# VectorE's and ScalarE's work in attention tied to program order, with three steps moved

## The chip, the cores and the metric

The kernel runs on one core of one Trainium2 chip. The metric is the device time of one execution in microseconds. The kernel before takes 2076.37 us (median of three runs, 2076.05 to 2076.4). The engines are named as in the profile: PE is TensorE (matrix products), DVE is VectorE, ACT is ScalarE, POOL is GpSimd, SP is the queue that starts DMA transfers. PSUM is the memory that TensorE writes its products to; it is divided into banks of 128 x 512 f32.

## The reference

The input x has 2048 rows of 640 numbers. Two kinds of layer alternate, each twice, each added to what went into it:

```
x = x + A(layernorm(x));  x = x + B(layernorm(x))
x = x + A(layernorm(x));  x = x + B(layernorm(x))

A(x):  a = x @ hid_re.T;  b = x @ hid_im.T           # Fourier transform over the columns
       y = seq_re @ a - seq_im @ b                   # and over the rows, real part
B(x):  q, k, v = x @ wqkv                            # 32 heads of 20
       s = q @ k.T * 20 ** -0.5
       s = where(0 <= row - col < 256, s, -1e9)      # each row sees itself and the 255 rows before it
       o = softmax(s) @ v;  return o @ wo
```

The Fourier matrices are inputs; A is computed as plain matrix products.

## The kernel before, in words

Large products are made of f16 parts: each operand is split into a high and a low f16 half, and three products of halves are added in PSUM. The program runs four stages, one after the other: spectral 0, attention 0 (555.8 to about 1073 us of the profiled span), spectral 1, attention 1 (from 1580.2 us to the end).

**Attention's loop.** It turns over pairs of heads and row tiles (`for G in range(NS // 2 + 1)`); one turn is called a visit here. There are 128 visits with scores, and a short tail. In a visit TensorE makes, in this order:

- the far scores of four heads of a 128-row tile (the key tile that lies two tiles back; 4 products into `sk`), which are needed for their maxima only;
- the transposed scores (`by_key`, key rows on the partitions) of the pair that was scored 8 visits ago, 12 products into the rest of `sk`; the exponential reads these, and by now they contain the negated row maximum as two more rows of the product;
- the near scores (8 products into `sq`);
- in even visits the two transposes of `back`, which turn a finished block of outputs (12 visits after its scores), and in odd visits one transpose of `hand_on` (the maxima of two visits as rows, 3 visits later) and the 32 products with v (`values`, 11 visits later);
- one unit of other work of 15 products: a projection of q, k or v, or a tile of the output product with wo. Units are 256 or 320 columns wide. A planner with due times chooses which.

VectorE's part is `largest(G, pi)` for pi 0 and 1, a copy and a reduce each: the copy (L1155) writes the far scores over those near ones that the mask takes out, so that one reduce (L1157) finds the maximum over all 256 columns. `back` adds a reciprocal (L1258, of the sums) and a multiply (L1259, into `o`) in even visits. ScalarE's part is `probabilities`, two exponentials (L1210, first pi = 1, then pi = 0), and copies out of PSUM: `ht` (L1175, the turned maxima, then sent to memory and back into the rows of q), `pvs` (L1242, the products with v), `qf` (L365) and `v` (L881, projections). GpSimd masks the exponentials and splits into halves.

In the background there are slow steps, one in an even visit and two in an odd one: the norm of rows for a later block (`norm_steps`: statistics L139 and L142, a square root by small operations on 128 x 1 numbers L148 to L152, the norm `lny` L166), ScalarE's f16 copy of it (L177, `rx`), and, in attention 0, the split of wo. The out tile adds into x by VectorE (L935).

**Where it lies in PSUM.** `sq` is one bank for each pi, `sk` two banks for each pi. The far scores are the first 256 columns of `sk`, the transposed scores the other 768, so that far scores and a part of the exponential's input share a bank. A ring of two banks (`pf`) serves everything else: back, hand_on, values and the units. Each waits until the reader of the bank two turns earlier is through.

**What sets the order.** TensorE's instructions and SP's transfers follow the order in which the program writes them (`tensor` and `load` chain them with `tc.issue_after` while `in_turn[0]` holds, that is in attention). GpSimd's are put in order by the scheduler. So are VectorE's and ScalarE's, but for a few ties: `in_line("dve")` ties each copy and each reduce, and the first operation of `back`, behind the last of VectorE's marked instructions, `in_line("act")` does the same for the exponentials, and a slow step comes behind the visit's last reduce (`topped`).

Of the kernel before, what the change touches and what calls it, by code (L numbers as in the profile page):

```python
# [72 lines left out]
def body(ctx: ExitStack, tc: tile.TileContext, x_in, cmat, whid, wqkv, wo, out):  # L73
# [55 lines left out]

    matmul, transpose = partial(tensor, "matmul"), partial(tensor, "transpose")  # L130

    def norm_steps(xs, ys, act=False):
# [3 lines left out]
        for k, x in enumerate(xs):  # L136
            st = keep.tile([P, 2, 6], F32, tag="lnst", name="lnst", bufs=2)
            for h in range(2):
                nc.vector.bn_stats(st[:, h], x[:, h * 320:(h + 1) * 320])  # L139
                if h == 0:  # L140
                    yield
            nc.vector.bn_aggr(mv[:, k], st.rearrange("p a b -> p (a b)"))  # L142
            yield
        t = keep.tile([P, 3, n], F32, tag=f"lnt{n}", name="lnt", bufs=2)
        ts = nc.vector.tensor_scalar
# [14 lines left out]
        for k, x in enumerate(xs):  # L160
            g, u = t[:, 1, k:k + 1], t[:, 2, k:k + 1]
            y = keep.tile([P, D], F32, tag="lny", name="lny", bufs=2)
            if act:
                nc.scalar.activation(y, x, AF.Identity, bias=u, scale=g)
# [11 lines left out]
    def split(hi, lo, y, eng):  # L176
        nc.scalar.activation(hi, y, AF.Copy)  # L177
        eng.tensor_tensor(lo, y, hi, op=OP.subtract)
# [45 lines left out]
    class Hidden:  # L224
# [29 lines left out]
        def stage(self, s, pool, new=new_f):  # L254
# [23 lines left out]
            def parts(m, f):  # L278
                nc.scalar.activation(zc[:, m, 0], f, AF.Copy)
                nc.gpsimd.tensor_tensor(zc[:, m, 1], f, zc[:, m, 0], op=OP.subtract)  # L280

            def scaled(o):
                nc.scalar.activation(o, z, AF.Copy, scale=Z_DOWN)

            def minus(o, f):
                nc.vector.scalar_tensor_tensor(o, z, Z_DOWN, f, op0=OP.mult, op1=OP.subtract)
# [42 lines left out]
    class Projections:  # L329
# [19 lines left out]
        def qk(self, b, w, ct):  # L349
# [15 lines left out]
            nc.scalar.activation(f, pf[:, :QB], AF.Copy, scale=down)  # L365
# [13 lines left out]
    def spectral(layer, res_src, hidden, first):  # L379
        with ExitStack() as st:  # L380
# [40 lines left out]
            def split_w(n, f):  # L421
                c, dt = divmod(n, ND)
                up = -C_UP if c else C_UP
                marks["act"] = nc.scalar.activation(w[:, 0, c, dt], f, AF.Copy, scale=up).ins
                marks["dve"] = nc.vector.scalar_tensor_tensor(w[:, 1, c, dt], f, up, w[:, 0, c, dt],
                                                              op0=OP.mult, op1=OP.subtract).ins

            def transposed(xs, k, xt):
# [3 lines left out]
                if k:  # L432
                    nc.vector.tensor_copy(xt[:, k], pt)
                else:
                    nc.scalar.activation(xt[:, k], pt, AF.Copy)
# [81 lines left out]
            def take_c(n):  # L517
# [13 lines left out]
                def high(m, f):  # L531
                    cc[m] = sb.tile([P, 2, RS * P], F16, tag="cc", name="cc", bufs=14)
                    nc.scalar.activation(cc[m][:, 0], f, AF.Copy, scale=C_UP)  # L533

                def low(m, f):
                    nc.vector.scalar_tensor_tensor(cc[m][:, 1], f, C_UP, cc[m][:, 0], op0=OP.mult, op1=OP.subtract)  # L536
# [21 lines left out]
            def add(o, z, f):  # L558
                marks["dve"] = nc.vector.scalar_tensor_tensor(o, z, Y_DOWN, f, op0=OP.mult, op1=OP.add).ins  # L559
# [12 lines left out]
            def main_a(r, j):  # L572
# [5 lines left out]
                marks["act"] = nc.scalar.activation(f[:, 0], z, AF.Copy, scale=Y_DOWN).ins  # L578
# [87 lines left out]
            def b_max():  # L666
# [3 lines left out]
                for n in range(20):  # L670
                    nc.vector.tensor_reduce(wmax[:, n:n + 1], fs[n], axis=AX.X, op=OP.max, apply_absolute_value=True)
# [5 lines left out]
            def b_scale():  # L677
                m2 = sb.tile([P, 2], F32, name="m2")
                nc.vector.tensor_reduce(m2[:, 0:1], wmax[:, :15], axis=AX.X, op=OP.max)
                nc.vector.tensor_reduce(m2[:, 1:2], wmax[:, 15:], axis=AX.X, op=OP.max)  # L680
# [4 lines left out]
                nc.vector.tensor_reduce(mr, pt[:2, :P], axis=AX.X, op=OP.max)  # L685
# [7 lines left out]
                nc.vector.tensor_scalar(e, mb, 2.0 ** -60, 2.0 ** 60, op0=OP.max, op1=OP.min)  # L693
                nc.vector.tensor_scalar(e.bitcast(I32), e.bitcast(I32), 0x7F800000, None, op0=OP.bitwise_and)
                nc.vector.tensor_scalar(wsc.bitcast(I32), e.bitcast(I32), -1, 0x7F000000, op0=OP.mult, op1=OP.add)
                nc.vector.tensor_scalar(wsc, wsc, W_UP, None, op0=OP.mult)
                nc.vector.tensor_tensor(alpha[:, 0:1], e[:, 0:1], e[:, 0:1], op=OP.mult)
                a = DH ** -0.5 / 64.0
                nc.vector.tensor_scalar(alpha[:, 1:2], alpha[:, 0:1], -a, None, op0=OP.mult)
                nc.vector.tensor_scalar(alpha[:, 0:1], alpha[:, 0:1], a, None, op0=OP.mult)  # L700
                nc.vector.tensor_tensor(beta, e[:, 0:1], e[:, 1:2], op=OP.mult)
# [731 lines left out]
```

## Time and profile before

| | |
|---|---|
| median of three runs | 2076.37 us |
| profiled execution | 2078.21 us, of which the span (first to last instruction) is 2076.4 us |
| granted TensorE clock, mean | 0.998 |
| attention 0, visits 0 to 127 | 555.77 to 1029.69 us |
| attention 1, visits 0 to 127 | 1580.21 to 2032.37 us |
| exponentials (L1210) | 512, 469.3 us in all |
| reduces (L1157) | 512, 345.4 us in all |
| mask copies from far scores (L1155) | 448, 189.7 us in all |

A row of the timeline gives the start in us from the span's start, the duration, the engine, the line, the operation with output and inputs by the program's names, shapes, how many instructions were joined to one row, and in brackets the engine's idle time ahead of it and what ended it. A row of the waits reads: engine, tile and line that waited, what it waited for, us in all, times, longest. A row of a group gives the busy time, the mean of one in ns, and the idle time ahead.

### The profile page before, as it was taken

The numbers are of one execution on the slowest core, as the hardware profiler recorded it, in microseconds if no ns is written. First come the engines' busy times: TensorE is split into PE (matmuls) and PEld (weight loads), VectorE is DVE, ScalarE is ACT, GpSimd is POOL, SyncE is SP. The second block draws the span as 40 slices with busy tenths as digits, with TensorE's granted clock in tenths as the row PEclk, the third lists the DMA queues.
The fourth block names the chain that finished last, engine by engine and source line by source line (L and its number), as shares of the span: only waits on it lengthen the run. The fifth ranks groups of instructions, "written<-read, shape, count | busy, mean of one in ns | idle before, by whom it ended". The sixth has DMA issues, their size and how long they took to land.

```text
span 2076.4 us, 55961 instructions
## 1 busy us (share of the span) xinstructions
PE 1996.0 (96%) x21881; PEld 1452.4 (70%) x21881; DVE 1552.9 (75%) x3261; ACT 1114.1 (54%) x1971; POOL 1471.0 (71%) x2162
## 2 busy tenths in 40 slices
PE   7999999999999999999999999999999999999998
PEld 4777777776767776777667777777677677777765
DVE  8888778767688788766638779787777877776673
ACT  5444555534256666666654444444342666666664
POOL 5777788868458778765557778777783677776654
PEclk9999999999999999999999999999999999999999
DMA  7556467565554444443635455454845454543322
GB/s 271 182 200 207 159 216 237 169 254 193 141 107 118 109 109 117 98 102 91 175 131 175 159 174 183 149 171 144 298 146 131 92 124 106 128 110 88 85 74 71
DMA packets 280509, 311.11 MB, mean 150 GB/s; under 512 B 107572, under 2 KB 214836, under 8 KB 271156
## 3 DMA queue, kind: packets, MB, share of 16 engines
q1 hardware_dynamic: 279668, 306.88, 49.9%
q8 instruction: 171, 2.80, 0.6%
q14 instruction: 94, 0.77, 0.1%
q10 hardware_dynamic: 576, 0.66, 0.1%
HBM read 201.72 MB, written 83.46 MB: 137 GB/s over the span
## 4 chain that ended last, share of the span: by engine, by line
PE 63%; DVE 16%; issue 6%; ACT 5%; POOL 5%; DMA 4%; SPq 0%; DVEq 0%; POOLq 0%; ACTq 0%
PE pf L126 28%; PE y L126 11%; PE x L126 10%; PE z L126 7%; PE sk L126 5%; DVE cc L536 4%; DVE sq L1155 3%; DVE m L1157 2%; ACT ptq L1210 2%; PE sq L126 2%; DMA res<-accd 2%; DVE res L559 1%; DVE lnt L151 1%; POOL cs L526 1%; DVE lnst L139 1%
## 5 line engine op out<-in xcount | busy, mean ns | idle before, releaser
L126 PEld LDWEIGHTS <-cc 128*128 128x128 f16 x5376 | 524.4, 98 | 214.8 <-issue 15.1
L1210 ACT ACTIVATE ptq<-sk,shift,alpha 128x768 f32<-128x768 f32 (+2 forms) x512 | 469.3, 944 | 111.0 <-DVE x L935 55.0
L126 PEld LDWEIGHTS <-big 128*128 128x128 f16 x4320 | 415.0, 98 | 129.6 <-issue 29.5
L1157 DVE TENSOR_REDUCE m<-sq 128x2 f32<-128x512 f32 (+1 forms) x512 | 345.4, 675 | 25.8
L1155 DVE COPY_PREDICATED sq<-mask,sk 128x256 f32<-128x256 int32 x448 | 189.7, 423 | 144.4 <-PE sq L126 138.1
L533 ACT ACTIVATE cc<-cs 128x512 f16<-128x512 f32 x256 | 153.6, 623 | 262.6 <-POOL cs L526 150.3
L126 PE MATMUL pf<-early,big 128*128 128x256 f16 x2400 | 289.2, 274 | 4.4 <-ACT ht L1175 3.7
L1214 POOL TENSOR_SCALAR_AFFINE_SELECT ptq<-ptq 128x512 f32<-128x512 f32 x224 | 144.3, 644 | 183.1 <-ACT ptq L1210 180.8
L126 PE MATMUL y<-zc,cc 128*128 128x320 f16 x1728 | 262.8, 299 | 3.2 <-DVE pf L559 3.2
L536 DVE SCALAR_TENSOR_TENSOR cc<-cs,cc 128x512 f16<-128x512 f32 x256 | 248.1, 978 | 6.9 <-ACT cc L533 6.8
L536 DVE SCALAR_TENSOR_TENSOR cc<-cq,cc 128x512 f16<-128x512 f32 x192 | 207.1, 1080 | 0.1
L126 PE MATMUL pf<-ptq,v 128*32 128x128 f32 (+1 forms) x3840 | 183.6, 329 | 10.1 <-DVE o L1259 3.5
L126 PE MATMUL z<-zc,cc 128*128 128x320 f16 x1152 | 177.7, 299 | 7.0 <-DVE res L559 7.0
L126 PE MATMUL x<-zc,cc 128*128 128x320 f16 x1152 | 177.7, 299 | 0.0
L1216 POOL TENSOR_SCALAR_AFFINE_SELECT ptq<-ptq 128x512 f32<-128x512 f32 x256 | 164.9, 644 | 13.0 <-ACT ptq L1210 12.8
L126 PEld LDWEIGHTS pf<-ptq,v 128*32 128x32 f32 x3840 | 114.8, 110 | 56.0 <-PE pf L126 7.7
L365 ACT ACTIVATE qf<-pf 128x256 f32<-128x256 f32 x160 | 60.9, 381 | 166.7 <-PE pf L126 128.7
L126 PE MATMUL pf<-big,early 128*128 128x320 f16 x960 | 141.0, 299 | 2.2 <-ACT ht L1175 1.3
L525 POOL TENSOR_TENSOR cs<-cq 128x512 f32<-128x512 f32 x64 | 86.6, 1354 | 69.8 <-DVE cc L536 69.1
L126 PEld LDWEIGHTS <-qs 62*128 62x128 f16 x2688 | 87.7, 94 | 59.1 <-issue 57.9
L126 PE MATMUL pf<-bo,ot 128*128 128x320 f16 x840 | 123.5, 299 | 4.6 <-DVE x L935 2.6
L126 PEld LDWEIGHTS <-ot 128*128 128x128 f16 x960 | 91.9, 98 | 46.6 <-issue 9.4
(141 smaller groups left out, 3505.4 us busy)
## 6 DMA issues: line engine op xcount, KB each, us to landing
cq<-in_cmat_dram SPq DMA_DIRECT2D x64, 1024.0 KB
accd<-res SPq DMA_DIRECT2D x96, 320.0 KB
res<-accd SPq DMA_DIRECT2D x96, 320.0 KB
x<-x2d SPq DMA_DIRECT2D x64, 320.0 KB
qkd<-early SPq DMA_DIRECT2D x160, 128.0 KB
ks<-qkd SPq DMA_DIRECT2D x108, 160.0 KB
qs<-qkd SPq DMA_DIRECT2D x84, 160.0 KB
x2d<-res SPq DMA_DIRECT2D x32, 320.0 KB
```

The lines of the kernel that those rows point to most:

```text
L126: i = getattr(nc.tensor, what)(*args, **kw)
L139: nc.vector.bn_stats(st[:, h], x[:, h * 320:(h + 1) * 320])
L151: ts(u, g, g, h, op0=OP.mult, op1=OP.mult)
L365: nc.scalar.activation(f, pf[:, :QB], AF.Copy, scale=down)
L525: g.tensor_tensor(s1, a21, a22, op=OP.add)
L533: nc.scalar.activation(cc[m][:, 0], f, AF.Copy, scale=C_UP)
L536: nc.vector.scalar_tensor_tensor(cc[m][:, 1], f, C_UP, cc[m][:, 0], op0=OP.mult, op1=OP.subtract)
L1155: marks["dve"] = nc.vector.copy_predicated(near[pi][:, :, 0], mask[:, None, :].to_broadcast([P, 2, P]), far).ins
L1157: marks["dve"] = nc.vector.tensor_reduce(TOP[n][:, pi, :, k], near[pi][:, :, :1 + (i >= 1)], axis=AX.XY, op=OP.max).ins
L1210: marks["act"] = nc.scalar.activation(o[:, pi], tps[pi][:, :, first:], AF.Sigmoid, bias=shift, scale=alpha[:, 0:1]).ins
L1214: nc.gpsimd.affine_select(out=q[:, :, a0], in_=q[:, :, a0], pattern=[[0, 4], [-1, P]], base=0, channel_multiplier=1, compare_op=OP.is_gt, ...
L1216: ins = nc.gpsimd.affine_select(out=q[:, :, a0 + 2], in_=q[:, :, a0 + 2], pattern=[[0, 4], [1, P]], base=0, channel_multiplier=-1, compare ...
```

## The change

A class `Pinned` wraps VectorE and ScalarE. Each of their instructions that the program issues while `in_turn[0]` holds is tied behind the one issued before it on the same engine. Every call of `nc.vector` and `nc.scalar` that computes now goes through it, so that in a listing of the changed program all these instructions carry the line of the wrapper, L140. With the order written in the program now being the order of the engines, some statements are moved:

- `largest` is split into `masked` (the copy) and `largest` (the reduce). The copies of both pi stand first, and both reduces with `part_tops` stand last, behind `back`.
- `hand_on` (the `ht` copy) stands between the two exponentials instead of behind them.
- `back`'s multiply becomes a marked instruction.
- in `rows_norm` one more `yield` stands between the norm and the f16 copies, so that these come one slow step later.

```diff
+    class Pinned:
+        def __init__(self, engine):
+            self.engine, self.last = engine, None
+        def __getattr__(self, what):
+            def run(*args, **kw):
+                with ExitStack() as order:
+                    if in_turn[0] and self.last is not None:
+                        order.enter_context(tc.issue_after(self.last))
+                    i = getattr(self.engine, what)(*args, **kw)
+                self.last = i.ins if in_turn[0] else None
+                return i
+            return run
+
+    vector, scalar = Pinned(nc.vector), Pinned(nc.scalar)
...
                 yield from norm_steps(x2s, ys)
+                yield
                 for t, y in enumerate(ys):
...
-            def largest(G, pi):
+            def masked(G, pi):
                 i, p0 = place(2 * G)
+                far = farq[pi] if i >= 2 else neg[:, None, :].to_broadcast([P, 2, P])
+                with in_line("dve"):
+                    marks["dve"] = vector.copy_predicated(near[pi][:, :, 0], mask[:, None, :].to_broadcast([P, 2, P]), far).ins
+
+            def largest(G, pi):
...
-                far = farq[pi] if i >= 2 else neg[:, None, :].to_broadcast([P, 2, P])
-                with in_line("dve"):
-                    marks["dve"] = nc.vector.copy_predicated(near[pi][:, :, 0], mask[:, None, :].to_broadcast([P, 2, P]), far).ins
...
                 if g < NG:
-                    largest(G, 0)
+                    masked(G, 0)
                 if keyed:
                     probabilities(G - KEY_LAG, 1)
                 if g < NG:
-                    largest(G, 1)
-                    if G % 2:
-                        part_tops(G // 2)
-                if keyed:
-                    probabilities(G - KEY_LAG, 0)
+                    masked(G, 1)
                 n = due(G, HAND_LAG)
                 if n is not None:
                     hand_on(n)
+                if keyed:
+                    probabilities(G - KEY_LAG, 0)
                 n = due(G, BACK_LAG)
                 if n is not None:
                     with in_line("dve"):
                         back(n)
+                if g < NG:
+                    for pi in range(2):
+                        largest(G, pi)
+                    if G % 2:
+                        part_tops(G // 2)
```

How the change moves instructions is seen at three places. First, VectorE in an even visit with nothing else in it, and the odd visit behind it (attention 0, visits 96 and 97). `sq_6968` and `sk_6970` are the scores of pi = 0, `sq_6969` and `sk_6971` those of pi = 1. Before:

```order
L1155 COPY_PREDICATED sq_6968<-mask,sk_6970 128x256
L1157 TENSOR_REDUCE m<-sq_6968 128x2
L1155 COPY_PREDICATED sq_6969<-mask,sk_6971 128x256
L1157 TENSOR_REDUCE m<-sq_6969 128x2
L1258 RECIPROCAL r<-pf 128x8
L1259 TENSOR_TENSOR o<-pf,r 128x160
```

In the change:

```order
L140 COPY_PREDICATED sq_6968<-mask,sk_6970 128x256
L140 COPY_PREDICATED sq_6969<-mask,sk_6971 128x256
L140 RECIPROCAL r<-pf 128x8
L140 TENSOR_TENSOR o<-pf,r 128x160
L140 TENSOR_REDUCE m<-sq_6968 128x2
L140 TENSOR_REDUCE m<-sq_6969 128x2
```

The two copies follow each other, back's two operations have moved ahead of the reduces, and the reduces are last. The odd visit behind has only copy, copy, reduce, reduce.

Second, VectorE in a visit with an out add and a slow step of the norm (attention 0, visit 58). Before:

```order
L1155 COPY_PREDICATED sq_6968<-mask,sk_6970 128x256
L1157 TENSOR_REDUCE m<-sq_6968 128x2
L1155 COPY_PREDICATED sq_6969<-mask,sk_6971 128x256
L1157 TENSOR_REDUCE m<-sq_6969 128x2
L1258 RECIPROCAL r<-pf 128x8
L139 BN_STATS lnst<-x_10743 128x6
L1259 TENSOR_TENSOR o<-pf,r 128x160
L142 BN_AGGR lnmv<-lnst 128x2
L935 SCALAR_TENSOR_TENSOR x_10595<-pf,beta,x_10595 128x320
```

In the change:

```order
L140 COPY_PREDICATED sq_6968<-mask,sk_6970 128x256
L140 COPY_PREDICATED sq_6969<-mask,sk_6971 128x256
L140 RECIPROCAL r<-pf 128x8
L140 TENSOR_TENSOR o<-pf,r 128x160
L140 TENSOR_REDUCE m<-sq_6968 128x2
L140 TENSOR_REDUCE m<-sq_6969 128x2
L140 BN_STATS lnst<-x_10713 128x6
L140 BN_AGGR lnmv<-lnst 128x2
L140 SCALAR_TENSOR_TENSOR x_10725<-pf,beta,x_10725 128x320
```

The multiply no longer stands behind a step of the norm, and the out add into x stands behind the reduces and the whole step.

Third, ScalarE around the place where `ht` was late (attention 0, visits 46 to 47). Before:

```order
L1210 ACTIVATE ptq<-sk_6971,shift,alpha 128x2x384
L1210 ACTIVATE ptq<-sk_6970,shift,alpha 128x2x384
L881 ACTIVATE v<-pf 128x16x20
L177 ACTIVATE rx<-lny 128x640
L1210 ACTIVATE ptq<-sk_6971,shift,alpha 128x2x384
L1210 ACTIVATE ptq<-sk_6970,shift,alpha 128x2x384
L1175 ACTIVATE ht<-pf 16x128
L1242 ACTIVATE pvs<-pf 128x256
```

In the change:

```order
L140 ACTIVATE ptq<-sk_6971,shift,alpha 128x2x384
L140 ACTIVATE ptq<-sk_6970,shift,alpha 128x2x384
L140 ACTIVATE rx<-lny 128x640
L140 ACTIVATE ptq<-sk_6971,shift,alpha 128x2x384
L140 ACTIVATE ht<-pf 16x128
L140 ACTIVATE ptq<-sk_6970,shift,alpha 128x2x384
L140 ACTIVATE pvs<-pf 128x256
```

`ht` is between the exponentials in every odd visit now (before it stood there in most visits, and behind them in this one), and the f16 copy `rx` stands right behind the exponentials of visit 46 rather than ahead of those of visit 47 with `v` between. TensorE's order is the same but for the units, which the planner chooses anew since the norm's rows come a step later: visit 46 has an out unit in place of one for v, visit 14 of each layer has one unit fewer, and visit 92 three out units of 15 products instead of two.

93 lines of the change are left out of this document (47 added, 46 removed).

## The prediction

> **What bounds the kernel now.** I read the page's head first, then a table by stage, the chain of waits, and the timeline of undisturbed visits. (A "visit" is one turn of the attention loop, from one far-score product to the next; even and odd visits alternate, layers are 0 and 1.)
>
> ```profile
> span 2076.4 us, 55961 instructions
> PE 1996.0 (96%) x21881; PEld 1452.4 (70%) x21881; DVE 1552.9 (75%) x3261; ACT 1114.1 (54%) x1971; POOL 1471.0 (71%) x2162
> ```
>
> TensorE is busy 96% of the span, so only what makes TensorE wait counts. The table by stage below has, in each row: stretch, its length, then busy us of PE, PEld, DVE, ACT, POOL, the granted clock, DMA share, GB/s. Its eight stretches are, for each layer, visits 0-25 (ramp), 26-91, 92-113 and 114-127.
>
> ```profile
> 555.77:645.60 89.83, 79.91 (x927) 58.10 (x927) 73.25 (x171) 46.53 (x95) 53.82 (x112) 0.98 0.46 113
> 645.60:891.80 246.20, 239.44 (x3730) 178.15 (x3730) 195.85 (x486) 167.50 (x265) 188.81 (x409) 1.00 0.47 113
> 891.80:976.29 84.49, 82.52 (x1260) 60.54 (x1259) 54.96 (x117) 52.69 (x83) 50.82 (x117) 1.00 0.40 101
> 976.29:1029.69 53.40, 50.61 (x762) 35.58 (x762) 39.04 (x84) 33.73 (x53) 31.70 (x72) 1.00 0.49 132
> 1580.21:1663.97 83.76, 77.93 (x926) 57.07 (x926) 69.02 (x166) 41.70 (x89) 52.66 (x112) 1.00 0.41 95
> 1663.97:1906.36 242.39, 238.29 (x3731) 178.15 (x3731) 182.52 (x437) 165.31 (x261) 181.89 (x405) 1.00 0.45 109
> 1906.36:1990.83 84.47, 82.51 (x1259) 60.53 (x1259) 54.95 (x117) 52.68 (x83) 50.81 (x117) 1.00 0.40 102
> 1990.83:2032.37 41.54, 39.75 (x686) 29.26 (x686) 35.73 (x77) 30.00 (x44) 26.91 (x63) 1.00 0.22 59
> ```
>
> TensorE stands still 6.8 and 4.1 us in the long stretches (246.20 less 239.44; 242.39 less 238.29), 2.0 in each third one, and 9.9 and 5.8 in the ramps: all that better orders can win is some 30 us, and VectorE is far from full. Of the stall, the list of waits (us in total, times, longest) names these, the first three rows from layer 0's long stretch, the last two from its ramp:
>
> ```profile
> PE pf L126 <- ACT ht L1175: 1.8, 2, 0.9
> PE pf L126 <- DVE o L1259: 1.5, 4, 0.7
> PE pf L126 <- DVE x L935: 0.7, 3, 0.2
> ...
> PE sk L126 <- ACT ptq L1210: 3.3, 3, 1.6
> PE sq L126 <- DVE m L1157: 3.2, 5, 1.1
> ```
>
> Now an undisturbed pair of visits, in the timeline (start, duration, engine, operation):
>
> ```profile
> 1870.68 0.29 PE L126 MATMUL sk<-ks,qs 62*128 62x128 f16 x4
> 1871.14 0.39 PE L126 MATMUL sq<-ks,qs 62*128 62x128 f16 x8
> 1871.39 1.87 ACT L1210 ACTIVATE ptq<-sk,shift,alpha 128x768 f32<-128x768 f32 x2
> 1871.63 0.43 DVE L1155 COPY_PREDICATED sq<-mask,sk 128x256 f32<-128x256 int32 x1 [1.76 <-PE sq L126]
> 1872.16 0.69 DVE L1157 TENSOR_REDUCE m<-sq 128x2 f32<-128x512 f32 x1
> 1872.77 0.42 DVE L1155 COPY_PREDICATED sq<-mask,sk 128x256 f32<-128x256 int32 x1
> 1873.22 0.69 DVE L1157 TENSOR_REDUCE m<-sq 128x2 f32<-128x512 f32 x1
> 1873.83 0.20 DVE L1258 RECIPROCAL r<-pf 128x8 f32<-128x8 f32 x1
> 1873.87 0.29 PE L126 MATMUL sk<-ks,qs 62*128 62x128 f16 x4
> 1874.13 0.33 DVE L1259 TENSOR_TENSOR o<-pf,r 128x160 f32<-128x160 f32 x1
> 1874.32 0.39 PE L126 MATMUL sq<-ks,qs 62*128 62x128 f16 x8
> 1874.53 0.99 ACT L1210 ACTIVATE ptq<-sk,shift,alpha 128x768 f32<-128x768 f32 x1
> 1877.84 0.29 PE L126 MATMUL sk<-ks,qs 62*128 62x128 f16 x4
> ```
>
> The even visit lasts 3.19 us (1873.87 less 1870.68), the odd one 3.97. Counted from the visit's start, near scores begin at 0.46, copy 0 runs 0.95-1.38, reduce 0 1.48-2.17, copy 1 2.09-2.51, reduce 1 2.54-3.23; then reciprocal and multiply. An operation independent of the one ahead starts 0.08 before that ends (1872.77 against 1872.85), a dependent one 0.10 after it (1872.16 against 1872.06). Reduce 1 is what matters: the next visit's near scores write the same bank, their second product not until reduce 1 is through. Here it ends at 3.23, and the next near scores begin at 3.64: slack. Where the even visit has the shorter, 256-column unit, the slack is already nothing:
>
> ```profile
> 1892.15 0.28 PE L126 MATMUL sk<-ks,qs 62*128 62x128 f16 x4
> 1894.69 0.69 DVE L1157 TENSOR_REDUCE m<-sq 128x2 f32<-128x512 f32 x1
> 1894.93 0.28 PE L126 MATMUL sk<-ks,qs 62*128 62x128 f16 x4
> 1895.39 0.43 PE L126 MATMUL sq<-ks,qs 62*128 62x128 f16 x8
> 1899.26 0.23 PE L126 MATMUL sk<-ks,qs 62*128 62x128 f16 x2
> ```
>
> That visit takes 2.78 us; reduce 1 ends at 1895.38 and the near scores begin at 1895.39. The pair lasts 7.11 (1899.26 less 1892.15): its odd visit takes 4.33 instead of 3.97, since the multiply comes late for it.
>
> **What copy 1 waits for.** The change takes reduce 0 from between the copies. Would copy 1 then start at 1.30? It reads the far scores of its bank pair, and the exponential that stands ahead of it in the program reads the same banks. In this trace it once waits for just that (VectorE's row, then ScalarE's):
>
> ```profile
> 641.12 0.43 DVE L1155 COPY_PREDICATED sq<-mask,sk 128x256 f32<-128x256 int32 x1 [1.34 <-ACT ptq L1210]
> 640.11 1.85 ACT L1210 ACTIVATE ptq<-sk,shift,alpha 128x768 f32<-128x768 f32 x2
> ```
>
> The pair of exponentials began at 640.11; half of 1.85 later the first is through, and copy 1 starts 0.04 behind. So it is held by the first exponential of its own visit. In the undisturbed pair that one ends at about 1.70 (ScalarE's two run 0.71 to 2.58, each 0.99). Before, copy 1 came at 2.09 and the wait was free; now it decides. [...]
>
> **The change, part by part.** *Even visits, steady state.* New order: copy 0 0.95-1.38, copy 1 1.74-2.17, reciprocal 2.09-2.29, multiply 2.39-2.71, reduce 0 2.63-3.32, reduce 1 3.24-3.93, all by the durations and overlaps above. Reduce 1 ends 0.70 later than now, because 0.53 of reciprocal and multiply moved ahead of it and copy 1 left VectorE idle 0.36 (1.38 to 1.74), while reduce 0's 0.69 no longer hides that idle time. The next near scores' second product can start at 3.98, after a 3.18 visit it would at 3.69: TensorE waits 0.30; after a 2.78 visit, 0.70. Both ways an even visit costs 3.48, and a pair 3.48+3.97=7.45 where it was 7.16 or 7.11, the odd visit's lateness being paid already. Odd visits (no back): reduce 1 ends at 3.39, the next is wanted at 4.4: nothing.
>
> *Out adds.* The two 320-column adds into x read a bank that the odd visit's values need. Without anything between they end at 4.40, in time. But the slow steps of the norm now stand ahead of them in full:
>
> ```profile
> L935 DVE SCALAR_TENSOR_TENSOR x<-pf,beta,x 128x320 f32<-128x320 f32 x11 | 5.9, 533 | 0.0
> L139 DVE BATCH_NORM_STATS2 lnst<-x 128x6 f32<-128x320 f32 x24 | 10.7, 462 | 0.0
> L142 DVE BATCH_NORM_AGGREGATE lnmv<-lnst 128x2 f32<-128x12 f32 x12 | 2.4, 199 | 0.1
> L151 DVE TENSOR_SCALAR lnt<-lnt 128x1 f32<-128x1 f32 x36 | 9.7, 269 | 1.1
> L166 DVE TENSOR_SCALAR lny<-x,lnmv,lnt 128x640 f32<-128x640 f32 x12 | 8.9, 743 | 0.1
> ```
>
> A statistics step is 0.60 (0.46 and 0.20, overlapped), four of the small ones 1.0 with their gaps, a row's norm 0.65 net. In layer 0's long stretch nine of the 11 adds have such a step ahead, three of each kind: 6.75. In layer 1 seven: two, two and three: 5.15. If a later slack swallows them they cost 0; I take them whole, since the multiply (o) of the same visit already makes TensorE wait up to 0.7 by the waits above.
>
> *Long stretches.* 33 pairs of 7.45 are 245.85, which already contains no other stall: with the adds 252.6 against 246.20, **+6.4**; in layer 1 251.0 against 242.39, **+8.6**. What vanishes inside this sum are the waits for ht, o and x above: multiply ends at 2.71 instead of about 3.8, and ht is fixed between the exponentials.
>
> *Visits 92-113.* Seven even visits of 3.18 wait 0.30, two pairs with a 2.78 visit go from 7.11 to 7.45: together 2.8. The extra yield shifts the work units: one of the 320-column kind (2.20 of TensorE) goes from visit 14 to 92. **+5.0** in each layer.
>
> *Visits 114-127.* Five even visits of about 3.2 per layer wait 0.30; layer 1 has one more: **+1.5 and +1.9**.
>
> *Ramp.* Visits are short here, so that the alternating copies and reduces with their dependency gaps come late (the 3.2 for m above), and ScalarE's copy of a piece of wo ahead of the exponentials is 1.6 of the 3.3 for ptq. Program order puts that copy behind them, and a unit leaves visit 14 (the 2.2 counted at visit 92): I take **-5.0** in layer 0 and **-1.5** in layer 1, where the stall is 4 us smaller; between nothing and -9.9, -5.8, all the standstill there is.
>
> Tails and spectral stages keep their order: 0. Sum 6.4+8.6+5.0+5.0+1.5+1.9-5.0-1.5 = **+21.9**. It is made against the profiled execution (2078.21, span 2076.4), which is 1.8 above the runs' median of 2076.37; on the median it gives **2098**.
>
> **Rivals.** *Copy 1 free (faster).* If the exponential doesn't hold it, copy 1 runs at 1.30, reduce 1 ends at 3.50: no wait after 3.18 visits, 0.27 after 2.78 ones. That takes 0.30 and 0.43, some 0.35 in the mean, off the 51 even visits from 26 on, in two layers: 36, and 2 from the adds: 2060. It decides as soon as reduce 1 ends before 3.64. For it: nothing in VectorE's data needs the exponential. Against: the row at 641.12. 0.13.
>
> *The gains are larger than taken (no change).* All 11.9 of the adds hidden and the ramps' gain doubled to 13: 2080. For it: the two adds of one visit are partly late already today. 0.08.
>
> *GpSimd late (slower still).* Its order isn't tied and changes; it is busy 188.81 of 246.20. If a mask step or cast came late by 0.12 in each of 102 pairs: +12, 2110. 0.07.
>
> *No overlap of VectorE's operations.* [...] The rows disagree (start 0.08 before the end). As a mechanism of this kernel, where three such overlaps precede reduce 1, losing them makes it 0.24 later in 102 even visits: +24, 2122. 0.03.
>
> **How the numbers follow.** The forecast holds 0.69, by itself 2086 to 2110 (the adds' 11.9 at nothing below; the ramp gain at nothing and some GpSimd above). The range 2068 to 2114 takes in the second and third rivals and leaves out the first and the last, 0.16, and a few in a hundred of tails. A difference of 0.2% (4 us) is about what a measurement can tell from none. Faster 0.14, the same 0.09, slower 0.77.
>
> **What would show it.** In the changed trace: copy 1 idle about 0.36 with the exponential named as releaser; reduce 1 ending 3.9 after an even visit's start; near scores waiting for m, 0.3 after 320-column units, 0.7 after 256 ones, and a pair of 7.45; no waits for ht; adds late where a slow step is ahead. Wrong: copy 1 starting at 1.30, clean pairs of 7.15, or the ramps losing time.

## The result and the profile after

The changed kernel takes 2100.89 us (median of four runs, 2100.09 to 2101.34), the one before 2076.39 (2076.05 to 2077.19): slower by 24.5 us, a ratio of 1.0113 with a 95% interval of 1.0098 to 1.0128. The forecast was 2098, 21.9 more.

The head of the page after:

```profile
span 2099.3 us, 55806 instructions
PE 2009.2 (96%) x21881; PEld 1448.9 (69%) x21881; DVE 1528.1 (73%) x3261; ACT 1128.3 (54%) x1971; POOL 1469.0 (70%) x2162
```

The span grew by 22.9. The instructions of each engine are as many as before; VectorE is even busy for 24.8 us less, mainly because independent instructions stand next to each other more often and overlap (two reduces in a row take 1.28, one alone 0.69). There is no more work than before, so the loss is in TensorE's waits and, in layer 1's ramp, in a stretch of lowered clock (see "Without the extra yield"). The same table by stage as in the prediction (visits 0-25, 26-91, 92-113, 114-127 of each layer; length, busy us of PE, PEld, DVE, ACT, POOL, granted clock, DMA share, GB/s):

```profile
554.91:640.67 85.76, 77.27 (x912) 56.39 (x912) 69.89 (x170) 45.79 (x93) 53.64 (x111) 0.98 0.45 110
640.67:894.96 254.29, 242.83 (x3731) 177.25 (x3731) 190.17 (x486) 173.80 (x267) 188.73 (x411) 1.00 0.49 110
894.96:984.67 89.71, 86.21 (x1274) 61.90 (x1274) 53.44 (x118) 53.60 (x82) 50.69 (x116) 1.00 0.40 102
984.67:1039.66 54.99, 52.33 (x761) 35.48 (x762) 37.86 (x84) 34.26 (x53) 31.54 (x72) 1.00 0.46 131
1590.81:1672.22 81.41, 77.01 (x911) 56.17 (x910) 65.32 (x166) 42.14 (x88) 51.57 (x112) 0.98 0.40 94
1672.22:1925.03 252.81, 242.53 (x3730) 177.29 (x3730) 177.15 (x436) 170.49 (x262) 181.92 (x406) 1.00 0.48 107
1925.03:2014.76 89.73, 86.23 (x1275) 61.90 (x1275) 53.41 (x118) 53.93 (x82) 50.74 (x116) 1.00 0.37 95
2014.76:2057.31 42.55, 41.28 (x686) 28.80 (x686) 34.50 (x77) 30.27 (x44) 26.60 (x63) 1.00 0.21 58
```

Against the table of before:

| stage | forecast, layers 0 and 1 | measured |
|---|---|---|
| ramp, visits 0-25 | -5.0, -1.5 | -4.1, -2.4 |
| visits 26-91 | +6.4, +8.6 | +8.1, +10.4 |
| visits 92-113 | +5.0, +5.0 | +5.2, +5.3 |
| visits 114-127 | +1.5, +1.9 | +1.6, +1.0 |
| all else (spectral stages, tails) | 0 | -2.3 |
| sum | +21.9 | +22.9 |

Of the -2.3, 2.0 are the tail behind visit 127 of layer 1 (41.99 against 44.03), in which the kernel before had a granted clock of 0.95 and the change 1.00.

In a busy time of PE that grew from 238.29 to 242.53 a part of the stall is hidden: a group of near scores that stops in the middle is shown as one long row. An undisturbed pair (visits 98 and 99 of layer 0) in the timeline after:

```profile
922.85 0.29 PE L126 MATMUL sk<-ks,qs 62*128 62x128 f16 x4
923.56 1.87 ACT L140 ACTIVATE ptq<-sk,shift,alpha 128x768 f32<-128x768 f32 x2
923.78 0.43 DVE L140 COPY_PREDICATED sq<-mask,sk 128x256 f32<-128x256 int32 x1 [1.90 <-PE sq L126]
924.59 0.43 DVE L140 COPY_PREDICATED sq<-mask,sk 128x256 f32<-128x256 int32 x1 [0.38 <-ACT ptq L140]
924.92 0.20 DVE L140 RECIPROCAL r<-pf 128x8 f32<-128x8 f32 x1
925.23 0.33 DVE L140 TENSOR_TENSOR o<-pf,r 128x160 f32<-128x160 f32 x1
925.47 1.28 DVE L140 TENSOR_REDUCE m<-sq 128x2 f32<-128x512 f32 x2
926.03 0.28 PE L126 MATMUL sk<-ks,qs 62*128 62x128 f16 x4
926.49 0.69 PE L126 MATMUL sq<-ks,qs 62*128 62x128 f16 x8
930.31 0.29 PE L126 MATMUL sk<-ks,qs 62*128 62x128 f16 x4
```

Copy 1 starts at 1.74 from the visit's start, after 0.38 of idle time that the exponential ended. Reduce 1 ends at 3.90 (925.47 + 1.28 - 922.85; the forecast said 3.93). The next near scores take 0.69 where they took 0.39: the missing 0.30. The pair lasts 7.46 (forecast 7.45). Where the even visit has a 256-column unit the wait is long enough to be split off as a row of its own (visit 107, 0.39); these near scores take 0.98 in all, 0.59 more than undisturbed ones, where the forecast said 0.70:

```profile
956.00 0.21 PE L126 MATMUL sq<-ks,qs 62*128 62x128 f16 x1
956.60 0.38 PE L126 MATMUL sq<-ks,qs 62*128 62x128 f16 x7 [0.39 <-DVE m L140]
```

The waits of TensorE in layer 0's visits 26 to 91, and then in layer 1's (us in all, times, longest):

```profile
PE pf L126 <- DVE x L140: 5.7, 9, 0.7
PE sq L126 <- DVE m L140: 3.5, 9, 0.4
```

```profile
PE pf L126 <- DVE x L140: 4.4, 7, 0.7
PE sq L126 <- DVE m L140: 3.5, 9, 0.4
```

The waits for `ht` and `o` are gone, and nine and seven late adds have come, as many as were counted. One of them, in visits 44 and 45 of layer 0:

```profile
711.38 1.28 DVE L140 TENSOR_REDUCE m<-sq 128x2 f32<-128x512 f32 x2
712.57 0.14 DVE L140 TENSOR_SCALAR lnt<-lnmv 128x1 f32<-128x1 f32 x1
712.75 0.72 DVE L140 TENSOR_SCALAR lnt<-lnt 128x1 int32<-128x1 int32 x3
713.38 0.54 DVE L140 SCALAR_TENSOR_TENSOR x<-pf,beta,x 128x320 f32<-128x320 f32 x1
713.98 1.51 PE L126 MATMUL pf<-ptq,v 128*32 128x256 f32 x32 [0.74 <-DVE x L140]
```

Two reduces, four small operations of the norm, then the add, and the values wait for it.

### The profile page after: what moved, and what is told of

It is laid out like the page before. It is cut to its first block, busy times and chain, and to the rows that moved or that the text cites. A ratio compares the mean times of both kernels' runs of the same rounds, so it can differ in the third digit from the quotient of the medians.

```text
span 2099.3 us, 55806 instructions
## 1 busy us (share of the span) xinstructions
PE 2009.2 (96%) x21881; PEld 1448.9 (69%) x21881; DVE 1528.1 (73%) x3261; ACT 1128.3 (54%) x1971; POOL 1469.0 (70%) x2162
## 4 chain that ended last, share of the span: by engine, by line
PE 62%; DVE 20%; ACT 7%; issue 4%; DMA 4%; POOL 2%; SPq 0%; DVEq 0%; ACTq 0%; POOLq 0%
PE pf L126 27%; PE y L126 11%; PE x L126 10%; PE z L126 7%; DVE m L140 6%; ACT ptq L140 5%; PE sk L126 4%; DVE cc L140 3%; DVE sq L140 3%; PE sq L126 2%; DVE lnt L140 2%; DVE o L140 1%; DMA res<-accd 1%; DVE res L140 1%; DVE big L140 1%
## 5 line engine op out<-in xcount | busy, mean ns | idle before, releaser
L140 ACT ACTIVATE ptq<-sk,shift,alpha 128x768 f32<-128x768 f32 (+2 forms) x512 | 471.6, 946 | 131.0 <-PE sk L126 55.0
L140 DVE COPY_PREDICATED sq<-mask,sk 128x256 f32<-128x256 int32 x448 | 185.9, 427 | 206.3 <-PE sq L126 150.9
L140 DVE TENSOR_REDUCE m<-sq 128x2 f32<-128x512 f32 (+1 forms) x512 | 318.9, 663 | 0.1
L140 ACT ACTIVATE cc<-cs 128x512 f16<-128x512 f32 x256 | 153.6, 624 | 261.8 <-POOL cs L543 149.5
L140 DVE SCALAR_TENSOR_TENSOR cc<-cs,cc 128x512 f16<-128x512 f32 x256 | 248.0, 978 | 7.5 <-ACT cc L140 7.4
L140 DVE SCALAR_TENSOR_TENSOR cc<-cq,cc 128x512 f16<-128x512 f32 x192 | 204.6, 1067 | 0.1
L126 PEld LDWEIGHTS <-qs 62*128 62x128 f16 x2688 | 93.3, 94 | 92.5 <-issue 86.9
L140 ACT ACTIVATE qf<-pf 128x256 f32<-128x256 f32 x160 | 61.0, 382 | 171.6 <-PE pf L126 83.0
L126 PEld LDWEIGHTS pf<-ptq,v 128*32 128x32 f32 x3840 | 109.3, 110 | 56.9 <-DVE x L140 12.6
L126 PE MATMUL sq<-ks,qs 62*128 62x128 f16 x1792 | 110.0, 216 | 19.1 <-DVE m L140 12.8
```

The lines of the kernel that those rows point to most:

```text
L126: i = getattr(nc.tensor, what)(*args, **kw)
L140: i = getattr(self.engine, what)(*args, **kw)
```

## The experiments

Theory: in even visits the end of reduce 1 sets the time, and it is late because reciprocal and multiply stand ahead of it and copy 1 waits for the exponential; to this come adds behind whole steps of the norm, and a unit that the extra yield moved to visit 92. Rivals: the ties themselves cost the time; VectorE's total work does; the wait of copy 1 costs nothing. Each group of four was run beside the kernel before, whose medians there were 2076.03, 2075.22 and 2075.48 (2076.39 beside the change), so a comparison across groups is good to about a microsecond. None of the variants leaves out a part of the computation.

### Back behind the reduces

```diff
-                n = due(G, BACK_LAG)
-                if n is not None: ... back(n)
                 if g < NG: ... largest(G, 0); largest(G, 1) ...
+                n = due(G, BACK_LAG)
+                if n is not None: ... back(n)
```

> The change with back's reciprocal and multiply behind the two reduces (copy, copy, reduce, reduce, reciprocal, multiply); all else tied as in the change. Theory (the end of reduce 1 in even visits sets the time): it ends at about 3.37 instead of 3.90 from the visit's start, so near scores wait nothing after a 320-column unit and about 0.1 after a 256-column one; pairs without an add go from 7.46 to about 7.16. Of 102 even visits some 84 have no late add: 84 times 0.30 is 25, so about 2076 (2072 to 2081). The late adds stay, their visits gain nothing. Rival (the ties themselves cost the time, since the scheduler can no longer fill VectorE's and ScalarE's gaps): 2095 or more, pairs stay near 7.4.

Measured: 2082.84 us, 1.0038 of before (1.0027 to 1.0048). Undisturbed pairs are 7.15 to 7.24; pairs with a late add stay at 8.1 to 8.4. So putting two instructions of 0.53 together behind the reduces gives back 18 of the 24.5 us, with every tie left in place: the rival on the ties falls. It misses the expected 2076 by 7, and the range by 2: many pairs gain less than 0.30, the median pair of the long stretches being 7.23. Rows of the pair at visits 98 and 99 of layer 0, and the start of the next pair:

```profile
913.75 0.28 PE L126 MATMUL sk<-ks,qs 62*128 62x128 f16 x4
915.83 1.28 DVE L140 TENSOR_REDUCE m<-sq 128x2 f32<-128x512 f32 x2
917.39 0.39 PE L126 MATMUL sq<-ks,qs 62*128 62x128 f16 x8
920.91 0.29 PE L126 MATMUL sk<-ks,qs 62*128 62x128 f16 x4
```

Reduce 1 ends 3.36 after the visit's start, the near scores of visit 99 begin at 3.64 and take 0.39, and the pair lasts 7.16.

### The order of before, tied

```diff
-  masked(G, 0); probabilities(.., 1); masked(G, 1); hand_on; probabilities(.., 0); back; largest(G, 0); largest(G, 1)
+  masked(G, 0); largest(G, 0); probabilities(.., 1); masked(G, 1); largest(G, 1); hand_on; probabilities(.., 0); back
```

> The change with the order of the statements of before (copy 0, reduce 0, copy 1, reduce 1, then back), but still all tied, ht between the exponentials, the extra yield kept: what the ties and the other two moves do without the moved copies and reduces. Theory: clean pairs are 7.15 again and near scores wait for nothing; late adds, the unit moved to visit 92 and the gain in the ramps stay as in the change: 2072 to 2079. Rival (ties cost the time): 2095 or more.

Measured: 2082.35 us, 1.0027 (1.0018 to 1.0036). The order of copies and reduces is worth 18.5 us by itself. It takes the same time as back behind the reduces (2082.84), where copy 1 still waits for the exponential (idle time of 0.37 in the row at 922.64 there): without back ahead of the reduces that wait costs nothing that can be measured. The result is 3 above the expected range; what remains above before lies in the long stretches (247.05 and 244.91 against 246.20 and 242.39, the late adds) and in visits 92-113 (87.4 against 84.5, the moved unit).

### Copies ahead of the exponentials

```diff
-  masked(G, 0); probabilities(.., 1); masked(G, 1); hand_on; probabilities(.., 0); back; largest ...
+  masked(G, 1); masked(G, 0); probabilities(.., 1); hand_on; probabilities(.., 0); back; largest ...
```

> The change with both copies written ahead of the exponentials (copy 1, copy 0, exponentials, back, reduces), so that no copy waits for an exponential of its visit, and the exponentials wait for the copies instead. Theory (the 0.38 that copy 1 waits for the exponential is part of the lateness): copies run 0.95 to 1.73, reduce 1 ends at 3.46, near scores wait nothing after a 320-column unit; ScalarE is 0.7 later, so that the next far scores wait about 0.15 for the exponentials. Pairs of about 7.30: 2085 (2080 to 2092). Rival (the copies' wait is idle time that costs nothing, back ahead of the reduces does it all): no better than the change, 2101 or more, since ScalarE's lateness comes on top.

Measured: 2132.37 us, 1.0267 (1.0252 to 1.0282): worse than the change by 31, far above the expected range and inside the rival's number. The timeline (visits 98 and 99 of layer 0) tells why:

```profile
933.96 0.29 PE L126 MATMUL sk<-ks,qs 62*128 62x128 f16 x4
934.90 0.76 DVE L140 COPY_PREDICATED sq<-mask,sk 128x256 f32<-128x256 int32 x2 [2.25 <-PE sq L126]
935.42 1.87 ACT L140 ACTIVATE ptq<-sk,shift,alpha 128x768 f32<-128x768 f32 x2 [0.90 <-DVE sq L140]
936.11 1.28 DVE L140 TENSOR_REDUCE m<-sq 128x2 f32<-128x512 f32 x2
937.79 0.40 PE L126 MATMUL sq<-ks,qs 62*128 62x128 f16 x8
938.77 0.99 ACT L140 ACTIVATE ptq<-sk,shift,alpha 128x768 f32<-128x768 f32 x1 [1.08 <-DVE sq L140]
939.66 0.25 ACT L140 ACTIVATE ht<-pf 16x128 f16<-16x128 f16 x1
```

VectorE does what theory said: the copies run back to back, reduce 1 ends at 3.43 (937.39 less 933.96), the near scores take 0.40, they wait for nothing. So copy 1's wait is a part of reduce 1's lateness. But now the exponentials wait for the copies (0.90 and 1.08) and all of ScalarE is 0.7 later. The waits of TensorE over the whole span:

```profile
PE sk L126 <- ACT ptq L140: 32.9, 60, 1.7
PE pf L126 <- ACT ht L140: 29.7, 74, 1.7
```

The first was expected (0.15 in a visit), the second forgotten: `ht` stands between the exponentials, so it is as late as they are, and the unit of the odd visit waits 0.31 for its bank. Pairs are 7.73.

### Without the extra yield

```diff
                 yield from norm_steps(x2s, ys)
-                yield
```

> The change without the extra yield in the norm of rows. Theory: it only moves work units; visit 92 has two out units again (6.0 instead of 8.86, 2.8 in each layer), and visit 14 gets its unit back, which costs there up to 2: 2097 to 2100. Rival (the yield is what lets the f16 copy find its norm done and so saves time on ScalarE): slower than the change, 2103 or more.

Measured: 2094.32 us, 1.0080 (1.0063 to 1.0097), so 6.6 less than the change (6.2 less when each is compared with the kernel before beside it), and below the expected range. Visits 92-113 fall from 89.71 and 89.73 to 86.87 and 86.88, the 2.8 in each layer. And the unit that comes back to visit 14 costs nothing in layer 0. Visits 14 and 15 of layer 0 in the change:

```profile
601.62 0.40 PE L126 MATMUL sk<-ks 62*128 62x128 f16 x8 [0.46 <-ACT ptq L140]
602.86 0.71 PE L126 MATMUL sq<-ks 62*128 62x128 f16 x8 [0.84 <-DVE m L140]
604.47 3.27 PE L126 MATMUL pf<-early,big 128*128 128x256 f16 x15
```

and without the yield:

```profile
598.97 1.80 PE L126 MATMUL pf<-early,big 128*128 128x256 f16 x15
600.70 0.40 PE L126 MATMUL sk<-ks 62*128 62x128 f16 x8
600.93 0.61 PE L126 MATMUL sq<-ks 62*128 62x128 f16 x8
```

With the unit in visit 14, the exponentials and reduces of that visit go on under it, and the next scores start without a wait. Without it TensorE stands there anyway, and then the unit of visit 15 takes 3.27 us where its 15 products take 1.80 elsewhere: the clock was lowered in this execution. Visit 15 of both layers in the table of stretches, of the change and then without the yield (length, busy us, in the third last column the granted clock):

```profile
601.62:607.67 6.05, 5.09 (x49) 3.10 (x49) 4.54 (x13) 2.07 (x4) 2.94 (x8) 0.72 0.84 222
1633.90:1639.50 5.60, 4.91 (x48) 3.02 (x47) 4.23 (x12) 2.09 (x4) 2.84 (x8) 0.70 0.41 141
```

```profile
600.70:604.02 3.32, 3.31 (x49) 2.32 (x49) 1.44 (x5) 2.19 (x5) 2.27 (x5) 1.00 0.90 248
1631.11:1634.26 3.15, 3.15 (x50) 2.33 (x50) 1.23 (x3) 2.20 (x5) 2.02 (x4) 1.00 0.55 141
```

In layer 0 visits 14 and 15 together take 7.93 us without the unit (599.74 to 607.67) and 6.31 with it (597.71 to 604.02). In layer 1 it hangs on the clock: with it lowered they take 7.05 without the unit, against 5.94 with it. The two kernels with one more instruction (below) have the change's program up to visit 25, and in layer 1 a clock of 1.00 in visit 15; there the two visits take 5.67 without the unit, so it costs 0.27.

### The slow steps behind the unit

```diff
-                for _ in range(STEPS[layer][G % 2]):
-                    slow_step()
                 ... run_unit ...
+                for _ in range(STEPS[layer][G % 2]):
+                    slow_step()
```

> The change with the slow steps of a visit written behind the unit of other work instead of ahead of it, so that an out add stands ahead of the norm's step of its visit. Nothing else moves on VectorE; TensorE's order is the same. Theory: the values' waits for x (5.7 and 4.4 us in the two long stretches of the change) go, near scores wait as in the change and pairs with an add are 7.5 as well: 2090 (2087 to 2094). Rival (the slow steps only move on and make the next copies late, by as much): 2098 or more.

Measured: 2099.10 us, 1.0118 (1.0101 to 1.0135): hardly less than the change. In the long stretches the theory holds for the adds: their pairs fall from 8.1-8.7 to 7.55-7.60 (one to 7.90) and the waits for `x` vanish; the stretches take 249.50 and 249.42 against 254.29 and 252.81. But four other pairs in each layer grow to 7.84 or 7.97, where the two steps of an odd visit now end late, which is the rival's mechanism; it takes a part of the gain. Of the 8.2 us that the long stretches gain, the profile shows 3.2 lost in the ramps and 3.2 outside the loop; whether these belong to the order or to this execution the one profile does not tell.

### The moved statements without the ties

```diff
-    vector, scalar = Pinned(nc.vector), Pinned(nc.scalar)
+    vector, scalar = nc.vector, nc.scalar
```

> The moved statements alone: the change without the ties of Pinned (only the ties that the kernel before had, which fix the order of copies, back's first operation and reduces), with the extra yield. Theory (the moved reduces cost the time, not the ties): the order of VectorE in undisturbed visits is the same as in the change, so near scores wait as there and pairs are 7.45; the adds stand inside a step of the norm instead of behind it and are less late, by some 5 us in all: 2093 to 2099. Rival (the ties cost the time): within 5 of before, 2081 or less.

Measured: 2100.98 us, 1.0123 (1.0108 to 1.0138), the change's time, slightly above the expected range and 20 from the rival's. Undisturbed pairs are 7.46. The moved statements do the harm with or without ties.

### The ties, without moved reduces and yield

```diff
-  the change's order, with the yield
+  masked(G, 0); largest(G, 0); probabilities(.., 1); masked(G, 1); largest(G, 1); hand_on; probabilities(.., 0); back
+  (no yield)
```

> Ties alone, nearly: order of statements of before for copies and reduces, all of VectorE and ScalarE tied, ht between the exponentials, no extra yield. By the runs before, the yield costs 6 (2100.9 against 2094.3) and this order gives back 18 (2100.9 against 2082.4). Theory (both are independent): 2076 (2073 to 2079), which is the kernel before, since the late adds eat what the freed waits for o and ht give. Rival (ties cost or save by themselves): 2084 or more, or 2070 or less.

Measured: 2075.03 us, 1.0003 (0.9992 to 1.0014). The two effects add up as expected, and the ties with the moved `ht` are worth nothing that can be measured: the pairs that waited for `ht` and `o` are 7.1 to 7.2 (visit 46 was 8.45), but most of those with an add are 7.9 to 8.3 (7.4 to 7.9 before). This is a balance: in the profiled executions the long stretches are 3.2 longer than before (247.87 and 243.94), and the ramps 5.4 shorter, some of it at a clock that was lowered before (0.98 in layer 0's ramp) and is 1.00 here.

### The same with the slow steps behind the unit

```diff
+  the kernel above, with the edit "slow steps behind the unit"
```

> The same with the slow steps behind the unit as well: ties, order of before, ht between the exponentials, no yield, out adds ahead of the norm's steps. Theory: in visits with an add the pair falls from about 8.2 to 7.4, 16 times 0.75 is 12: 2064 (2060 to 2068), faster than both kernels. Rival (the steps of the norm only get in the way of the next copies): 2074 or more.

Measured: 2080.02 us, 1.0027 (1.0015 to 1.0038). The theory fails, and the result is in the rival's range. Most pairs with an add fell to 7.47-7.88, but five pairs in layer 0 and four in layer 1 grew to 7.7-8.2, among them one with an add in each. The long stretches gain 2.6 and 0.7 against the kernel above. The profiled execution then loses 12.4 in layer 0's ramp (97.45 against 85.04, with a granted clock of 0.95 and a wait of 2.9 for a transfer). But it is the slowest of the ten runs (2088.49), so that ramp does not stand for the median, and where the median loses its 5 us is open.

### Slow step behind the unit in even visits only

```diff
-                for _ in range(STEPS[layer][G % 2]):
-                    slow_step()
+                if G % 2:
+                    for _ in range(STEPS[layer][G % 2]):
+                        slow_step()
                 ... run_unit ...
+                if G % 2 == 0:
+                    for _ in range(STEPS[layer][G % 2]):
+                        slow_step()
```

> Ties, order of before for copies and reduces, ht between the exponentials, no yield, and the slow step behind the unit in even visits only (there the out adds are; the two steps of an odd visit stay ahead of its unit). Theory: the pairs with an add fall from 8.1 to 7.5 as they did with all steps moved, and the pairs that grew there to 7.8 and 8.1 because odd visits' steps came late stay at 7.15: 2069 (2065 to 2073), faster than both kernels. Rival (moving a step only moves the lateness): 2075 or more.

Measured: 2071.04 us, 0.9970 of before (0.9959 to 0.9981): in the expected range and faster than both kernels, by 4.4 us against the one before. The long stretches are 244.84 and 240.76 (before 246.20 and 242.39; with the steps ahead of the unit 247.87 and 243.94). Pairs with an add are 7.47 to 7.87 in layer 0: the adds are nearly out of the way, and the steps of odd visits were left where they fit.

### One more instruction in even visits, or in odd ones

```diff
+                if G % 2 == 0 and 26 <= G < NG // 2:          # the other kernel: G % 2 == 1
+                    spare = sb.tile([P, P], F32, tag="spare", name="spare", bufs=2)
+                    with in_line("dve"):
+                        marks["dve"] = vector.tensor_tensor(spare, neg, neg, op=OP.mult).ins
                 if g < NG:
                     for pi in range(2):
                         largest(G, pi)
```

> The change with one more VectorE instruction in each even visit from 26 to 126 of both layers, just ahead of the reduces: a 128x128 multiply of constants into a tile that nobody reads (so it adds work and changes no result). By the 128x160 multiply's 0.33 and the overlap of 0.08 it makes reduce 1 some 0.2 later. Theory (the end of reduce 1 in even visits sets the time from 26 on): 102 times 0.2 is 20: 2121 (2114 to 2127). Rival (VectorE has room, the change's loss is elsewhere): 2101 to 2105.

> The same instruction in the odd visits from 27 to 127 instead, just ahead of the reduces: as much more work for VectorE. Theory: in odd visits reduce 1 has 0.7 and more to spare, so it costs nothing but in the few short odd visits behind 113: 2101 to 2104. Rival (VectorE's total work sets the time): as much as in even visits, 2114 or more.

Measured: 2120.96 us in even visits (1.0217, 1.0202 to 1.0232), 20.1 above the change; 2102.65 in odd ones (1.0128, 1.0111 to 1.0145), 1.8 above it, both as expected. The group of the added instruction (shortest, median and longest ns, first and last start) and the pair at visits 102 and 103 with it:

```profile
L140 DVE TENSOR_TENSOR spare<-neg x102: 281/282/725, 645.1 to 2071.7; 128x128 f32<-128x128 f32 x102
```

```profile
942.35 0.28 DVE L140 TENSOR_TENSOR spare<-neg 128x128 f32<-128x128 f32 x1
942.55 1.28 DVE L140 TENSOR_REDUCE m<-sq 128x2 f32<-128x512 f32 x2
943.89 0.38 PE L126 MATMUL sq<-ks,qs 62*128 62x128 f16 x7 [0.30 <-DVE m L140]
```

It takes 0.28 and pushes the reduces by 0.20; 102 times 0.20 is 20.4. Clean pairs go from 7.46 to 7.66. The same instruction in odd visits is as much work for VectorE and leaves undisturbed pairs at 7.46; the 1.8 us are too little to tell from nothing.

### The yield alone

```diff
  (the kernel before)
                 yield from norm_steps(x2s, ys)
+                yield
```

> The kernel before with the extra yield alone. Theory: it moves a unit from visit 14 to 92 in each layer, which costs 2.8 there and gives nothing back in the ramp, whatever the order of VectorE's work: 2081 (2079 to 2084). Rival (it costs only together with the ties): 2074 to 2078.

Measured: 2084.15 us, 1.0042 (1.0028 to 1.0056). It costs without ties too, by 8.7 with an interval from 5.8 to 11.6, a little above the expected range. Visits 92-113 are 86.5 in each layer instead of 84.5, so 4.1 of it is the unit that came to visit 92. Where the rest of the median lies is open: the profiled execution is the fastest of the five, and its ramps (89.3 and 83.1) are no longer than before's. In layer 0's it waits for a transfer that was covered before:

```profile
PE pf L126 <- DMA x<-x2d: 2.8, 1, 2.8
```

## Why the prediction was right, and where a step was off

**The wait of copy 1 and the end of reduce 1: right.** Forecast 1.74 and 3.93, measured 1.74 and 3.90; the pair 7.45 against 7.46. (In the row at 641.12 the first exponential ends at 641.08, 0.03 ahead of copy 1; the half of 1.85 in the forecast's working puts it at 641.04.) The waits of VectorE in layer 0's long stretch name the exponential 33 times, as often as there are even visits:

```profile
DVE sq L140 <- ACT ptq L140: 11.8, 33, 0.7
```

In the same stretch of the kernel before they name it twice:

```profile
DVE sq L1155 <- ACT ptq L1210: 1.0, 2, 0.6
```

That the exponential would hold copy 1 in every even visit was the author's estimate from the row at 641.12; the trace after agrees, with idle time of 0.38 ahead of copy 1 in the undisturbed pair. In that pair's odd visit copy 1 follows copy 0 with no idle time between them that the timeline sets apart: both copies are one row of 0.91 from 927.24, and the first exponential (0.99 from 926.69) ends at 927.68, where copy 0 ends at 927.67. The rival "copy 1 free" is out by the trace. That the end of reduce 1 in even visits sets the time is shown, not only argued: 0.20 more there in 102 visits costs 20, as much in odd visits 1.8, and taking back's 0.53 from ahead of it gives 18 back.

**Late adds: right in number, a little small in size.** Nine and seven, forecast at 6.75 and 5.15 above the pairs' 7.45. The nine pairs together are 74.6, 7.5 above nine times 7.46, the seven 6.0 above. That is 1.6 of the 3.5 us by which visits 26 to 91 are longer than forecast. The term that was most too small is the norm of a row, taken at 0.65: its three pairs in layer 0 are 8.31, 0.85 above. The rest sits in pairs that the sum took as clean, such as visits 26 and 56 of layer 0 (7.81 and 7.79): in the first pair the odd visit has a 320-column unit, in the second copy 1 starts at 2.07 instead of 1.74.

**Ramp and yield: the sum near, one of its steps wrong.** The prediction set the unit that left visit 14 against the one that came to visit 92, as part of the ramp's gain. Visit 92 is longer by 2.84 (8.86 against 6.02; the forecast took 2.20, and 2.8 for the waits of visits 92-113, which came to 2.4), but the unit's leaving saved nothing on the whole: without the yield the ramps are 82.6 and 81.7 against the change's 85.8 and 81.4. The step failed because it took TensorE's time in visit 14 for the bound where the exponential and the reduces were: a unit between them was covered. The clock of visit 15, which the forecast left out, comes on top (layer 0: 0.72 without the unit, 1.00 with it). So the yield is worth some 6 us of the loss and not about zero. That the ramps came near their -5.0 and -1.5 is luck: without the yield they are 7.2 and 2.1 shorter than before, in whose layer 0 a lowered clock (0.72 in visit 14) is a part of the length.

**The sum: nearer than its terms.** +21.9 against +22.9 is closer than the parts: the long stretches took 3.5 more than forecast, and the tail of layer 1 gave back 2.0 that no term had. In layer 1's last visits a pair grew by 0.15 (5.93 to 6.08) and not by 0.30.

**The rivals.** No overlap of VectorE's operations: out, two reduces in a row take 1.28 and not 2 x 0.69, and in the undisturbed pair the reciprocal starts at 924.92, 0.10 before copy 1 ends (925.02). GpSimd late: TensorE's waits in the long stretches name it nowhere. Gains larger than taken: the waits for `ht` and `o` are gone from the long stretches and the sum still came out higher than forecast; without the moved reduces and the yield, ties and moved `ht` together change nothing (2075.03 against 2075.22).

So of the 24.5 us some 18 to 19 come from the order of copies, back and reduces (2100.89 less 2082.35; 2094.32 less 2075.03), about 6 from the yield, and the ties add nothing that can be measured.

## What to carry to other kernels

An order written by hand is only as good as the question which instruction's end is waited for soonest: here two short instructions whose result is wanted a visit later were put ahead of one that was wanted at once, and filler work was taken from where it covered a wait. Before moving something, write down for each instruction on the engine when its reader wants it, and measure the slack by putting a dummy instruction there: 0.28 us, 102 times, cost 20 us in one place and 1.8 in the other. A wait that looks free (a copy behind an exponential that shares its bank) was free here only while there was slack behind it: with back's 0.53 behind the reduces it cost nothing that could be measured (2082.84 against 2082.35 us), with back ahead of them it became a part of the lateness.

## What the runs showed of the hardware that was not expected

**TensorE's clock is often lower behind short waits, but not always.** In the rows above, waits of 0.46 and 0.84 and the missing unit go with a granted clock of 0.72 in visit 15 (0.70 in layer 1), and 15 products of 256 columns take 3.27 us instead of 1.80. In layer 0, visit 15 has 0.50 to 0.74 in all nine profiled executions that have the yield (two of them also wait for a transfer there), and 1.00 in three of the four variants without; the fourth, 0.55, waited 2.9 in its ramp for a transfer, and the kernel before has 0.72 in visit 14 and 0.93 in 15 with the unit in place. In layer 1 only three of the nine have a lowered clock in visit 15 (0.69 to 0.74), and six have 1.00. Among the six are the two kernels with one more instruction, whose waits in visits 14 and 15 are the change's: 0.63, 0.26, 0.23 and 0.62 or 0.63. So the same short waits come with a lowered clock in one execution and not in another, and what decides is open. In visit 15 of layer 0 the change has 0.94 from 601.60 to 604.40 us, where the waits of 0.46 and 0.84 lie, and 0.53 from 604.40 to 607.70, behind them. The link is one of coincidence; no run forced such a wait by itself.

**The time follows the granted clock in small steps.** Over the 52 runs of the kernel before that lie beside the three groups of experiments, those with a mean granted clock of 1.000 take 2073.7 us in the mean (14 runs) and those with 0.998 take 2077.4 (18 runs). That is as large as the smallest differences here, and a reason to compare medians of several runs. In the traces the lowered clock lies in the ramps and in the last tail: layer 0's ramp takes 82 to 97 us over the profiled kernels, while undisturbed pairs in the long stretches repeat to 0.01 us.
